# Loading wq on 128 partitions in two DMAs, and cutting each of the two last wo loads into four DMAs, in a decode attention kernel

## The chip, the core and the metric

The kernel runs on one core of a Trainium2 chip. The metric is the device time of one execution in microseconds (us); smaller is better. The core has a matrix engine (TensorE, PE in the profile, with its weight loads as PEld), a vector engine (VectorE, DVE), a scalar engine (ScalarE, ACT), GpSimd (POOL) and SyncE (SP), which here only issues DMAs. The engines run independently and meet at semaphores. Sixteen DMA engines carry the data from the memory of the chip (HBM) into the on-chip memory (SBUF, 128 partitions).

## What is computed

One decoding step: one token attends over a cache of 65,536 positions with 8 key/value heads and 16 query heads of 256 numbers each, and the result is mixed with a small token-mixing MLP by a sigmoid gate.

```python
g = sigmoid((x * gate_w).sum(-1))                # x: 1 x 1 x 448
q = (x @ wq).reshape(1, 1, 16, 256)              # wq: 448 x 4096
k, v = repeat(k_cache, 2), repeat(v_cache, 2)    # caches: 1 x 8 x 65536 x 256
p = softmax(q @ k.T / 16)
a = (p @ v).reshape(1, 1, 4096) @ wo             # wo: 4096 x 448
b = gelu(layernorm(x).T @ w1 + b1) @ w2 + b2     # over the token axis, of length 1
out = g * a + (1 - g) * b
```

Everything is bfloat16. The two caches are 268 MB each, the rest is small: wq and wo are 3.67 MB each.

## The kernel before, in words

The caches are read as NP = 64 pieces, j = 0 to 63, eight to a key/value head (PPH = 8). A piece is 8.39 MB of keys (tile kring) and 8.39 MB of values (tile vbuf), each on 128 partitions with 128 rows of 256 numbers per partition. Inside a piece PE works in BODY = 8 chunks: `transposes` (L293) turns the keys around with an identity matrix into PSUM (kst), DVE (L551) and ACT (L649) copy them to ktT, `scores` (L313) multiplies them by the two queries of the head, ACT makes the exponentials pT (L638), and after the eight chunks `values` (L348) multiplies pT by the values.

**The order of the loads** is written by hand in SP's program (L222 to L263). SP issues one DMA after the other; each is spread over the DMA engines, and each DMA engine works through its share of the queued DMAs in order. First comes wq (L223), into the space of vbuf, which no values need yet. Then, for j = 0, the two halves of the keys; then SP waits until the queries and the layer norm are ready (s_q, s_hb, L242 and L243) because the first values overwrite wq and other early tiles; then the values, and a wo load (L255). For every later j, SP waits until PE has transposed the first four chunks of the piece before (L232), issues keys j, waits until PE has finished with values j-1 (L245), and issues values j. The last piece comes in smaller DMAs: keys in two halves, values in rows 0 to 96, 96 to 112, 112 to 124 and 124 to 128. Each of these has its own semaphore. After them SP issues the two last wo loads (L258 to L260), one for each query head of the last key/value head: 128 partitions of two wo rows, 1,792 bytes per partition. SP then waits for the result (s_fin) and stores it.

**ACT's queue** issues the small loads at the start (L618 to L623): x, gate_w, w1, b1 and w2 (14 rows of 256 bytes each), and the single number b2.

**The start on the engines.** PE spreads x over partitions with four matmuls (L416), so that xcol[p, j] is x[4p + j]; this fits wq_a, in which partition p holds the four wq rows 4p to 4p+3, on PQ = 112 partitions. PE then waits for the small loads (L418), turns w1, b1 and w2 around (L419), DVE copies the result (L499, L500), and PE computes the queries with 16 x 2 groups of four matmuls (L428). DVE's layer norm and gate (L474 to L513) run beside it; DVE finishes with hbT (L588), which lets SP issue the first values.

**The end.** PE's `tail` (L401) adds the last value rows in `late_values`, waits for oTn from DVE, and then, for each of the two heads h, waits for that head's wo load (L408) and multiplies (L395, `project`). DVE adds up the output (L613) and SP stores it (L262).

Of the kernel before, what the change touches and what calls it, by code (L numbers as in the profile page):

```python
# [12 lines left out]
def bass_gated_mix__gqa_block_cached__mixer_token_mlp__decode_kernel(  # L13
# [14 lines left out]
    bf16 = mybir.dt.bfloat16  # L28
# [4 lines left out]
    DH = A_k_cache.shape[3]  # L33
    DM = A_x.shape[-1]
# [3 lines left out]
    FT = F // 128  # L38
    P = 128
    NQ = HQ * DH  # L40
# [13 lines left out]
    KTB = 2  # L54
    assert T % (CH * BODY) == 0 and PPH >= 2


    WF = 4
    PQ = DM // WF
    assert PQ * WF == DM and PQ <= P and PQ % 16 == 0  # L60

    NFIRST = 96
    NLATE = 112
    pieces = [(NFIRST, NLATE), (NLATE, 124), (124, NV)]


    NCG = 4
# [22 lines left out]
    with ctx:  # L92
        def sb(shape, dt, name):
            return ctx.enter_context(nc.sbuf_tensor(name, shape, dt))

        def psum(shape, dt, name):
            return ctx.enter_context(nc.psum_tensor(name, shape, dt))

        def new_sem(name):
            return ctx.enter_context(nc.semaphore(name))  # L100
# [9 lines left out]
        ident = sb([P, P], f32, "ident")  # L110
        ones_sq = sb([P, P], bf16, "ones_sq")

        wo_sb = sb([P, REP, 2 * DM], bf16, "wo_sb")
# [6 lines left out]

        early = vbuf[:, :, :].rearrange("p n d -> p (n d)")
        early_f = vbuf_f[:, :, :].rearrange("p n d -> p (n d)")
        wq_a = early[0:PQ, 0:WF * NQ].rearrange("p (j n) -> p j n", j=WF)
        used = [WF * NQ]

        def scratch(rows, n, dt=bf16):
            o = used[0]
            used[0] += n if dt == bf16 else 2 * n
            assert used[0] <= NV * DH and n % 2 == 0
            return early[0:rows, o:o + n] if dt == bf16 else early_f[0:rows, o // 2:o // 2 + n]  # L130

        wrows_b = scratch(3 * FT, P)
        identb = scratch(3 * FT, 3 * FT)
        xrow_b = scratch(1, DM)
        grow_b = scratch(1, DM)
        xcb_row = scratch(1, DM)
# [4 lines left out]
        scr_row = scratch(1, DM, f32)  # L141
        gu = sb([P, DM], bf16, "gu")
        w2cur = sb([P, 1], bf16, "w2cur")
        xcol = sb([PQ, WF], bf16, "xcol")
        oTn = sb([P, 2 * REP], bf16, "oTn")
        accs = sb([P, SELC], f32, "accs")
        sel = sb([P, REP], f32, "sel")
# [7 lines left out]
        params = sb([P, 3 * FT], f32, "params")  # L155
# [14 lines left out]
        sps = psum([P, 2, 512], f32, "sps")  # L170
        acc = psum([P, 512], f32, "acc")
# [8 lines left out]
        sem_wq = new_sem("sem_wq")  # L180
        sem_wo = new_sem("sem_wo")
        sem_wl = [new_sem("sem_wl%d" % h) for h in range(REP)]
# [6 lines left out]
        s_par = new_sem("s_par")  # L189
# [5 lines left out]
        s_d2a = new_sem("s_d2a")  # L195
        s_a2d = new_sem("s_a2d")
        s_col = new_sem("s_col")
        s_identb = new_sem("s_identb")
        s_xcol = new_sem("s_xcol")
        s_hrow = new_sem("s_hrow")  # L200
        s_h = new_sem("s_h")
# [14 lines left out]
        def src(cache, j, n0=0, n1=NV):  # L216
            g, m = divmod(j, PPH)
            s = cache[0, g, m * BODY * CH:(m + 1) * BODY * CH, :].rearrange("(p n) d -> p n d", p=P)
            return s[:, n0:n1, :].rearrange("p n d -> p (n d)")

        @block.sync
        def _(eng):  # L222
            eng.dma_start(wq_a.rearrange("p j n -> p (j n)"),  # L223
                          A_wq.rearrange("(p j) n -> p (j n)", j=WF)).then_inc(sem_wq, 16)
            def load(dst, cache, j, n0, n1, at, sem):
                eng.dma_start(dst[:, at + n0:at + n1, :].rearrange("p n d -> p (n d)"), src(cache, j, n0, n1)  # L226
                              ).then_inc(sem, 16)

            for j in range(NP):
                last = j == NP - 1  # L230
                if j >= 1:
                    eng.wait_ge(sem_tr[NB - 1], BODY * (j - 1) + DC)  # L232
                if j == 0:
                    load(kring, A_k_cache, j, HV, NV, 0, sem_k)
                    load(kring, A_k_cache, j, 0, HV, 0, sem_kb)
                elif last:
                    load(kring, A_k_cache, j, 0, HV, HV, sem_k)
                    load(kring, A_k_cache, j, HV, NV, HV, sem_kb)
                else:
                    load(kring, A_k_cache, j, 0, NV, HV * (j % 2), sem_k)  # L240
                if j == 0:
                    eng.wait_ge(s_q, 1)  # L242
                    eng.wait_ge(s_hb, 1)  # L243
                else:
                    eng.wait_ge(sem_pv, j)  # L245
                load(vbuf, A_v_cache, j, 0, NFIRST if last else NV, 0, sem_v)
                if last:
                    for (n0, n1), sem in zip(pieces, sem_vp):
                        load(vbuf, A_v_cache, j, n0, n1, 0, sem)
                g, m = divmod(j, PPH)  # L250
                if m == 0 and g < H - 1:
                    if g >= 1:
                        eng.wait_ge(s_proj, g)
                    w = A_wo[g * REP * DH:(g + 1) * REP * DH, :]
                    eng.dma_start(wo_rows, w.rearrange("(p i) n -> p (i n)", i=2 * REP)).then_inc(sem_wo, 16)  # L255

            eng.wait_ge(s_proj, H - 1)
            for h in range(REP):  # L258
                w = A_wo[(HQ - REP + h) * DH:(HQ - REP + h + 1) * DH, :]
                eng.dma_start(wo_sb[:, h, :], w.rearrange("(p j) n -> p (j n)", j=2)).then_inc(sem_wl[h], 16)  # L260
            eng.wait_ge(s_fin, 1)
            eng.dma_start(out_ap, out_g[0:P:P // NCG, :]).then_inc(sem_out, 16)  # L262
            eng.wait_ge(sem_out, 16)  # L263
# [13 lines left out]
        def _(pe):  # L277
            one = ones_sq[0:1, 0:1]
# [85 lines left out]
            def late_values(n0, n1):  # L364
                for n in range(n0, n1):
                    r, nt = divmod(n, NT)
                    piece_wait(n)
                    for dj in range(2):
                        ins = pe.matmul(sps[:, 0, dj * REP:(dj + 1) * REP], vbuf[:, n, dj:DH:2],
                                        pT[:, r, 2 * nt:2 * nt + 2], start=False,  # L370
                                        stop=(n == NV - 1), skip_group_check=True)
                return ins

            def by_d(dst):
                for dj in range(2):
                    ins = pe.matmul(dst[:, dj * REP:(dj + 1) * REP], accs[:, dj:DH:2], sel[:, :],
                                    start=(dj == 0), stop=True, skip_group_check=True)
                return ins
# [22 lines left out]
            def tail():  # L401
                pe.wait_ge(s_cp, H)
                by_d(sps[:, 0, 0:2 * REP])
                late_values(NLATE, NV).then_inc(s_late, 1)
                spin(1)
                pe.wait_ge(s_oTn, H)
                for h in range(REP):
                    pe.wait_ge(sem_wl[h], 16)  # L408
                    ins = project([dj * REP + h for dj in range(2)], 2 * h)
                ins.then_inc(s_proj, 1)  # L410

# [1 line left out]
            pe.wait_ge(sem_ident, 1)  # L413
            pe.wait_ge(sem_x, 16)
            for j in range(WF):
                pe.matmul(acc[0:PQ, j:j + 1], xrow_b[0:1, j:DM:WF], one, start=True, stop=True)  # L416
            pe.wait_ge(s_identb, 1)
            pe.wait_ge(sem_misc, 16 * 5)  # L418
            pe.matmul(acc[:, WF:WF + 3 * FT], wrows_b, identb, start=True, stop=True).then_inc(s_col, 1)  # L419

            pe.wait_ge(s_xcol, 1)
            pe.wait_ge(sem_wq, 16)
            for dj in range(2):
                for h in range(HQ):
                    j = dj * HQ + h
                    col = h * DH
                    for kt in range(WF):
                        ins = pe.matmul(sps[:, 1, j:j + 1], wq_a[:, kt, col + dj:col + DH:2],  # L428
                                        xcol[:, kt:kt + 1], start=(kt == 0), stop=(kt == WF - 1))
            ins.then_inc(s_q, 1)  # L430
            pe.wait_ge(s_hrow, 1)
            pe.matmul(prj[:, 0:DM], ones_sq[0:1, :], h_row, start=True, stop=True)  # L432
# [10 lines left out]
            with nc.Fori(0, H, 1, engines=on, head_slot={pe.engine: 0}) as g:  # L443
                with nc.Fori(0, PPH, 1, engines=on, head_slot={pe.engine: 0}) as m:
                    j = pe.snap(g * PPH + m, min_val=0, max_val=NP - 1)
# [19 lines left out]
        def _(vec):  # L465
            for b in range(0, NB, 2):
                vec.sem_inc(sem_ev[b], 1)
            vec.memset(zrow[:, :], 0.0)
            vec.wait_ge(sem_ident, 1)
            vec.tensor_copy(identb, ident[0:3 * FT, 0:3 * FT]).then_inc(s_identb, 1)  # L470
            vec.reduce_sum(sel[:, :], ident[:, :].rearrange("p (j n) -> p n j", j=4)[:, 0:REP, :], axis=AX.X)
            vec.wait_ge(sem_x, 16)
            vec.drain()
            vec.tensor_copy(xrow, xrow_b)  # L474
            vec.drain()
            vec.reduce_sum(stat[:, 0:1], xrow, axis=AX.X)
# [19 lines left out]
            vec.drain()  # L496
            vec.tensor_copy(statb[:, 4:5], stat[:, 3:4]).then_inc(s_d2a, 1)  # L497
            vec.wait_ge(s_col, 1)
            vec.tensor_copy(xcol[:, :], acc[0:PQ, 0:WF]).then_inc(s_xcol, 1)  # L499
            vec.tensor_copy(params[:, :], acc[:, WF:WF + 3 * FT]).then_inc(s_par, 1)  # L500
            vec.drain()
            vec.tensor_copy(w2p_b[:, :], params[:, 2 * FT:3 * FT])
            vec.wait_ge(s_a2d, 1)
# [87 lines left out]
            with nc.Fori(0, H - 1, 1, engines=on) as g:  # L591
                with nc.Fori(0, PPH, 1, engines=on) as m:
                    j = vec.snap(g * PPH + m, min_val=0, max_val=NP)
# [90 lines left out]
```

The softmax here doesn't subtract the row's maximum and nothing guards it: scores larger than these inputs give would overflow.

## Time and profile before

| | us |
|---|---|
| median of three executions | 1271.55 |
| lowest and highest of the three | 1271.47, 1271.93 |
| the profiled execution, its own time | 1271.93 |
| span of the profiled execution (first to last instruction) | 1270.1 |
| PE busy, of the span | 921.5 |
| ACT busy, of the span | 536.9 |
| DVE busy, of the span | 419.9 |
| HBM read | 544.22 MB, 428 GB/s over the span |

The profiled execution is the one that gave the highest of the three times; 1.8 us of its time lie outside its span. In the profile, L223 is line 223 of the kernel. A row "kring<-in_A_k_cache_dram" is a DMA from the key cache to the tile kring; "SPq" and "ACTq" are the issuing queues. The arrow in an idle time ("<-DMA ...") names what ended the wait. "Landing" is the arrival of a DMA's semaphore, which counts the DMA engines that have finished their share. The trace also keeps a record of each packet that a DMA engine moved (start, duration, size), and of each landing.

### The profile page before, as it was taken

The numbers are of one execution on the slowest core, as the hardware profiler recorded it, in microseconds if no ns is written. First come the engines' busy times: TensorE is split into PE (matmuls) and PEld (weight loads), VectorE is DVE, ScalarE is ACT, GpSimd is POOL, SyncE is SP. The second block draws the span as 40 slices with busy tenths as digits, with TensorE's granted clock in tenths as the row PEclk, the third lists the DMA queues.
The fourth block names the chain that finished last, engine by engine and source line by source line (L and its number), as shares of the span: only waits on it lengthen the run. The fifth ranks groups of instructions, "written<-read, shape, count | busy, mean of one in ns | idle before, by whom it ended". The sixth has DMA issues, their size and how long they took to land.

```text
span 1270.1 us, 38819 instructions
## 1 busy us (share of the span) xinstructions
PE 921.5 (73%) x17109; PEld 868.6 (68%) x17109; DVE 419.9 (33%) x752; ACT 536.9 (42%) x786; POOL 0.9 (0%) x7
## 2 busy tenths in 40 slices
PE   1776688666886667876677866769767688676798
PEld 1766688666786666776667866668766577666687
DVE  2323344333443334443223332223322233322233
ACT  0533355433454334554334543335533355433455
POOL 0000000000000000000000000000000000000000
PEclk9978898878887778988889888788878798878889
DMA  9999999999999999999999999999999999999998
GB/s 326 433 435 433 435 431 433 431 435 431 429 435 435 431 433 440 429 429 438 435 431 427 440 433 433 433 435 431 433 431 431 435 433 433 433 433 429 440 424 358
DMA packets 11470, 544.39 MB, mean 429 GB/s; under 512 B 1361, under 2 KB 1619, under 8 KB 2771
## 3 DMA queue, kind: packets, MB, share of 16 engines
q1 hardware_dynamic: 11368, 544.22, 99.7%
q8 instruction: 8, 0.13, 0.0%
q10 hardware_dynamic: 90, 0.01, 0.0%
q14 instruction: 4, 0.02, 0.0%
HBM read 544.22 MB, written 0.00 MB: 428 GB/s over the span
## 4 chain that ended last, share of the span: by engine, by line
DMA 69%; PE 29%; issue 1%; DVE 0%; ACTq 0%; SPq 0%; ACT 0%; DVEq 0%
DMA kring<-in_A_k_cache_dram 66%; PE kst L293 24%; PE sps L313 4%; DMA wo_sb<-in_A_wo_dram 2%; DMA b_b<-in_B_b_dram 2%; PE acc L348 0%; PE sps L428 0%; SPq L226 0%; ACTq L621 0%; DVE hbT L588 0%; DVE stat L495 0%; ACTq L618 0%; PE prj L432 0%; SPq L260 0%; DVE vbuf L493 0%
## 5 line engine op out<-in xcount | busy, mean ns | idle before, releaser
L649 ACT ACTIVATE ktT<-kst 128x1024 bf16<-128x1024 bf16 x512 | 499.1, 1021 | 662.4 <-PE kst L293 662.3
L293 PE MATMUL kst<-ident,kring 128*128 128x128 f32 x4096 | 559.7, 298 | 295.8 <-DMA kring<-in_A_k_cache_dram 284.6
L293 PEld LDWEIGHTS kst<-ident,kring 128*128 128x128 f32 x4096 | 509.8, 155 | 305.9 <-issue 303.2
L551 DVE COPY ktT<-kst 128x1024 bf16<-128x1024 bf16 x512 | 353.9, 692 | 756.4 <-PE kst L293 736.0
L313 PEld LDWEIGHTS sps<-qcur,ktT 128*128 128x128 bf16 x8192 | 237.7, 96 | 4.6 <-issue 2.1
L313 PE MATMUL sps<-qcur,ktT 128*128 128x2 bf16 x8192 | 236.6, 163 | 1.6 <-issue 1.5
L348 PE MATMUL acc<-vbuf,pT 128*2 128x256 bf16 x4080 | 148.9, 316 | 2.3 <-issue 1.5
L348 PEld LDWEIGHTS acc<-vbuf,pT 128*2 128x2 bf16 x4080 | 109.6, 96 | 33.0 <-issue 2.0
L638 ACT ACTIVATE pT<-sps 128x32 f32 x256 | 51.8, 202 | 16.6 <-PE sps L313 16.6
L337 PE MATMUL acc<-pT,ones_sq 128*128 128x32 bf16 x256 | 11.7, 178 | 12.3 <-ACT pT L638 12.3
L337 PEld LDWEIGHTS acc<-pT,ones_sq 128*128 128x128 bf16 x256 | 8.6, 97 | 15.2 <-ACT pT L638 14.9
L556 DVE COPY accs<-acc 128x288 f32<-128x288 f32 x8 | 3.7, 458 | 41.8 <-PE acc L348 41.8
L655 ACT ACTIVATE z_b<-z_b 128x448 bf16<-128x448 bf16 x14 | 8.1, 577 | 20.4 <-DVE z_b L538 20.4
L419 PE MATMUL acc<-vbuf 42*128 42x42 bf16 x1 | 0.2, 190 | 20.0 <-DMA b_b<-in_B_b_dram 20.0
L419 PEld LDWEIGHTS acc<-vbuf 42*128 42x128 bf16 x1 | 0.1, 102 | 20.0 <-issue 20.0
L384 PEld LDWEIGHTS acc<-sel,accs 128*64 128x64 f32 x112 | 10.8, 214 | 0.9
L384 PE MATMUL acc<-sel,accs 128*64 128x1 f32 x112 | 11.4, 260 | 0.0
L628 ACT ACTIVATE statb<-statb 1x1 bf16<-1x1 bf16 x1 | 0.2, 204 | 19.2 <-DVE statb L497 19.2
L493 DVE TENSOR_TENSOR vbuf<-vbuf 1x448 bf16<-1x448 bf16 x1 | 0.4, 381 | 16.8 <-DMA b_b<-in_B_b_dram 16.8
L544 DVE TENSOR_TENSOR gu<-wtmp,z_b 128x448 bf16<-128x448 bf16 x14 | 5.5, 393 | 1.0
L532 DVE TENSOR_TENSOR z_b<-wtmp,u_b 128x448 bf16<-128x448 bf16 x14 | 5.5, 393 | 1.0
L530 DVE TENSOR_TENSOR wtmp<-u_b 128x448 bf16<-128x448 bf16 x14 | 5.5, 392 | 1.1
(78 smaller groups left out, 81.1 us busy)
## 6 DMA issues: line engine op xcount, KB each, us to landing
kring<-in_A_k_cache_dram SPq DMA_DIRECT2D x4, 4096.0 KB, 27.2
vbuf<-in_A_v_cache_dram SPq DMA_DIRECT2D x1, 6144.0 KB, 24.7
vbuf<-in_A_wq_dram SPq DMA_DIRECT2D x1, 3584.0 KB, 17.5
wo_sb<-in_A_wo_dram SPq DMA_DIRECT2D x7, 448.0 KB, 27.2
vbuf<-in_A_v_cache_dram SPq DMA_DIRECT2D x1, 1024.0 KB, 26.9
vbuf<-in_A_v_cache_dram SPq DMA_DIRECT2D x1, 768.0 KB, 28.3
vbuf<-in_A_v_cache_dram SPq DMA_DIRECT2D x31, 29.7
kring<-in_A_k_cache_dram SPq DMA_DIRECT2D x30, 27.6
```

What stands on the lines that cost most here:

```text
L293: ins = pe.transpose(kst[:, b, i * P:(i + 1) * P], kring_f[:, at + NT * (k % DC) + 4 * b + i, :], ident[:, :])
L313: ins = pe.matmul(sps[:, par, 2 * nt:2 * nt + 2], ktT[:, par, b, ntl * DH + dj:(ntl + 1) * DH:2], qcur[:, dj, :], start=(dj == 0), stop=(d ...
L337: pe.matmul(acc[:, DENC:SELC], ones_sq[:, :], pT[:, r, :], start=False, stop=(r == BODY - 1), skip_group_check=True)
L348: ins = pe.matmul(acc[o:o + REP, 0:DH], pT[:, r, 2 * nt:2 * nt + 2], vbuf[:, n, :], start=False, stop=False, skip_group_check=True)
L384: ins = pe.matmul(dst[hh * HP:(hh + 1) * HP, i:i + 1], accs[:, i:DH:2 * REP], sel[:, hh:hh + 1], start=False, stop=True, skip_group_check= ...
L530: vec.tensor_tensor(W, U, U, op=ALU.mult)
L532: vec.tensor_tensor(Z, W, U, op=ALU.mult)
L544: vec.tensor_tensor(gu[:, :], W, Z, op=ALU.mult).then_inc(s_pb, 1)
L551: vec.tensor_copy(ktT[:, k % KTB, b, :], kst_b[:, b, :]).then_inc(sem_ev[b], 1)
L638: act.activation(pT[:, bass.ds(p0 + k % DC, 1), :].rearrange("p o n -> p (o n)"), sps[:, k % 2, 0:2 * NT], AF.Exp, scale=scale).then_inc(s ...
L649: act.activation(ktT[:, k % KTB, b, :], kst_b[:, b, :], AF.Copy).then_inc(sem_ev[b], 1)
L655: act.activation(z_b[:, :], z_b[:, :], AF.Tanh).then_inc(s_tanh, 1)
```

## The change

Two parts of the load program are different.

- **wq.** In place of one DMA to 112 partitions of four rows each, two DMAs: rows 0 to 383 go to 128 partitions of three rows each (wq_a, 24,576 bytes per partition), and the 64 rows that are left go to 128 partitions of half a row each (wq_b, 4,096 bytes per partition). A half row holds the columns of eight heads, so that each query head uses either the even or the odd partitions of wq_b: x is laid out for that in two more columns of xcol, with zeros on the other partitions. DVE fills a row xrem for this (one memset, two copies), PE spreads it with two more matmuls, and the fourth matmul of each group reads wq_b in place of the fourth row of wq_a. PE waits for both DMAs (32 in place of 16 on sem_wq).
- **wo.** Each of the two last wo loads is cut at partitions 96, 121 and 126 into four DMAs of 96, 25, 5 and 2 partitions. They run on 16, 5, 5 and 2 of the DMA engines, where the uncut load runs on 16 with 8 partitions each. All four count on the same semaphore, and PE waits for 64.

```diff
-    WF = 4
-    PQ = DM // WF
+    WF = 3
+    REM = DM - WF * P
+    HALF = NQ // 2
...
+    wo_cuts = [(0, 96), (96, 121), (121, 126), (126, P)]
...
-        wq_a = early[0:PQ, 0:WF * NQ].rearrange("p (j n) -> p j n", j=WF)
+        wq_a = early[:, 0:WF * NQ].rearrange("p (j n) -> p j n", j=WF)
+        wq_b = early[:, WF * NQ:WF * NQ + HALF]
+        xrem = scratch(1, 2 * P).rearrange("p (a n) -> p a n", a=2)
...
             eng.dma_start(wq_a.rearrange("p j n -> p (j n)"),
-                          A_wq.rearrange("(p j) n -> p (j n)", j=WF)).then_inc(sem_wq, 16)
+                          A_wq[0:WF * P, :].rearrange("(p j) n -> p (j n)", p=P)).then_inc(sem_wq, 16)
+            eng.dma_start(wq_b, A_wq[WF * P:DM, :].rearrange("r (a n) -> (r a) n", a=2)
+                          ).then_inc(sem_wq, 16)
...
                 w = A_wo[(HQ - REP + h) * DH:(HQ - REP + h + 1) * DH, :]
-                eng.dma_start(wo_sb[:, h, :], w.rearrange("(p j) n -> p (j n)", j=2)).then_inc(sem_wl[h], 16)
+                rows = w.rearrange("(p j) n -> p (j n)", j=2)
+                for p0, p1 in wo_cuts:
+                    eng.dma_start(wo_sb[p0:p1, h, :], rows[p0:p1, :]).then_inc(sem_wl[h], 16)
...
-                    pe.wait_ge(sem_wl[h], 16)
+                    pe.wait_ge(sem_wl[h], 16 * len(wo_cuts))
...
             for j in range(WF):
-                pe.matmul(acc[0:PQ, j:j + 1], xrow_b[0:1, j:DM:WF], one, start=True, stop=True)
-            pe.wait_ge(s_identb, 1)
+                pe.matmul(acc[:, j:j + 1], xrow_b[0:1, j:WF * P:WF], one, start=True, stop=True)
+            pe.wait_ge(s_xrem, 2)
+            for a in range(2):
+                pe.matmul(acc[:, WF + a:WF + a + 1], xrem[0:1, a, :], one, start=True, stop=True)
...
-            pe.wait_ge(sem_wq, 16)
+            pe.wait_ge(sem_wq, 32)
...
                     for kt in range(WF):
-                        ins = pe.matmul(sps[:, 1, j:j + 1], wq_a[:, kt, col + dj:col + DH:2],
-                                        xcol[:, kt:kt + 1], start=(kt == 0), stop=(kt == WF - 1))
+                        pe.matmul(sps[:, 1, j:j + 1], wq_a[:, kt, col + dj:col + DH:2],
+                                  xcol[:, kt:kt + 1], start=(kt == 0), stop=False)
+                    ins = pe.matmul(sps[:, 1, j:j + 1], wq_b[:, cb + dj:cb + DH:2],
+                                    xcol[:, WF + a:WF + a + 1], start=False, stop=True)
...
+            vec.memset(xrem, 0.0)
...
-            vec.tensor_copy(identb, ident[0:3 * FT, 0:3 * FT]).then_inc(s_identb, 1)
+            vec.tensor_copy(identb, ident[0:3 * FT, 0:3 * FT]).then_inc(s_xrem, 1)
...
+            vec.tensor_copy(xrem[0:1, 0, 0:P:2], xrow_b[0:1, WF * P:DM])
+            vec.tensor_copy(xrem[0:1, 1, 1:P:2], xrow_b[0:1, WF * P:DM]).then_inc(s_xrem, 1)
...
-            vec.tensor_copy(xcol[:, :], acc[0:PQ, 0:WF]).then_inc(s_xcol, 1)
+            vec.tensor_copy(xcol[:, :], acc[:, 0:WF + 2]).then_inc(s_xcol, 1)
```

More of the change, by code (lines that the diff above doesn't have):

```diff
@@ L55, in bass_gated_mix__gqa_block_cached__mixer_token_mlp__decode_kernel @@
     assert T % (CH * BODY) == 0 and PPH >= 2
-    WF = 4
-    PQ = DM // WF
-    assert PQ * WF == DM and PQ <= P and PQ % 16 == 0
+    WF = 3
+    REM = DM - WF * P
+    assert 0 < REM and 2 * REM == P
+    HALF = NQ // 2
     NFIRST = 96
@@ L122, in bass_gated_mix__gqa_block_cached__mixer_token_mlp__decode_kernel @@
         early_f = vbuf_f[:, :, :].rearrange("p n d -> p (n d)")
-        wq_a = early[0:PQ, 0:WF * NQ].rearrange("p (j n) -> p j n", j=WF)
-        used = [WF * NQ]
+        wq_a = early[:, 0:WF * NQ].rearrange("p (j n) -> p j n", j=WF)
+        wq_b = early[:, WF * NQ:WF * NQ + HALF]
+        used = [WF * NQ + HALF]
         def scratch(rows, n, dt=bf16):
@@ L143, in bass_gated_mix__gqa_block_cached__mixer_token_mlp__decode_kernel @@
         w2cur = sb([P, 1], bf16, "w2cur")
-        xcol = sb([PQ, WF], bf16, "xcol")
+        xcol = sb([P, WF + 2], bf16, "xcol")
         oTn = sb([P, 2 * REP], bf16, "oTn")
@@ L197, in bass_gated_mix__gqa_block_cached__mixer_token_mlp__decode_kernel @@
         s_col = new_sem("s_col")
-        s_identb = new_sem("s_identb")
+        s_xrem = new_sem("s_xrem")
         s_xcol = new_sem("s_xcol")
@@ L415, in _ @@
             for j in range(WF):
-                pe.matmul(acc[0:PQ, j:j + 1], xrow_b[0:1, j:DM:WF], one, start=True, stop=True)
-            pe.wait_ge(s_identb, 1)
+                pe.matmul(acc[:, j:j + 1], xrow_b[0:1, j:WF * P:WF], one, start=True, stop=True)
+            pe.wait_ge(s_xrem, 2)
+            for a in range(2):
+                pe.matmul(acc[:, WF + a:WF + a + 1], xrem[0:1, a, :], one, start=True, stop=True)
             pe.wait_ge(sem_misc, 16 * 5)
-            pe.matmul(acc[:, WF:WF + 3 * FT], wrows_b, identb, start=True, stop=True).then_inc(s_col, 1)
+            pe.matmul(acc[:, WF + 2:WF + 2 + 3 * FT], wrows_b, identb, start=True, stop=True).then_inc(s_col, 1)
             pe.wait_ge(s_xcol, 1)
-            pe.wait_ge(sem_wq, 16)
+            pe.wait_ge(sem_wq, 32)
             for dj in range(2):
@@ L426, in _ @@
                     col = h * DH
+                    a, cb = divmod(col, HALF)
                     for kt in range(WF):
-                        ins = pe.matmul(sps[:, 1, j:j + 1], wq_a[:, kt, col + dj:col + DH:2],
-                                        xcol[:, kt:kt + 1], start=(kt == 0), stop=(kt == WF - 1))
+                        pe.matmul(sps[:, 1, j:j + 1], wq_a[:, kt, col + dj:col + DH:2],
+                                  xcol[:, kt:kt + 1], start=(kt == 0), stop=False)
+                    ins = pe.matmul(sps[:, 1, j:j + 1], wq_b[:, cb + dj:cb + DH:2],
+                                    xcol[:, WF + a:WF + a + 1], start=False, stop=True)
             ins.then_inc(s_q, 1)
@@ L498, in _ @@
             vec.wait_ge(s_col, 1)
-            vec.tensor_copy(xcol[:, :], acc[0:PQ, 0:WF]).then_inc(s_xcol, 1)
-            vec.tensor_copy(params[:, :], acc[:, WF:WF + 3 * FT]).then_inc(s_par, 1)
+            vec.tensor_copy(xcol[:, :], acc[:, 0:WF + 2]).then_inc(s_xcol, 1)
+            vec.tensor_copy(params[:, :], acc[:, WF + 2:WF + 2 + 3 * FT]).then_inc(s_par, 1)
             vec.drain()
```

## The prediction

> **What bounds the kernel now.** I read the page from the top. Its slices by time come first:
>
> ```profile
> PEclk9978898878887778988889888788878798878889
> DMA  9999999999999999999999999999999999999998
> GB/s 326 433 435 433 435 431 433 431 435 431 429 435 435 431 433 440 429 429 438 435 431 427 440 433 433 433 435 431 433 431 431 435 433 433 433 433 429 440 424 358
> ```
>
> The DMA engines are busy in every slice of 31.75 us and move about 433 GB/s in each, while PE is busy 73% of the span. So the kernel is bound by the stream of loads, and its time is the start of the stream, plus the bytes at the rate, plus what follows the last landing. The first slice is odd: as busy as the others, but at 326 GB/s. The busy times by stretch resolve it (columns: stretch, its length, busy time of each engine with its instructions, PE clock, DMA share, GB/s):
>
> ```profile
> 2.00:15.00 13.00, 0.55 (x4) 0.49 (x4) 3.10 (x12) 1.28 (x1) 0.00 (x0) 1.00 0.98 253
> 15.00:18.00 3.00, 0.00 (x0) 0.00 (x0) 0.00 (x0) 0.00 (x0) 0.00 (x0) 1.00 0.84 252
> 18.00:30.00 12.00, 4.88 (x133) 3.97 (x133) 3.43 (x16) 1.69 (x3) 0.00 (x0) 1.00 1.00 431
> ```
>
> From 2 to 18 us the engines are occupied but run at 253 GB/s; from 18 us on they run at 431. The slow stretch is the wq load. In the trace's packet records, wq is 112 packets of 32,768 bytes, seven to an engine, started at 1.76 to 14.82 us, mean 2.03 us each. The first keys, which follow on the same engines, have packets of the same size: 1.22 us each. Key packets begun before 17.2 us are still slow, those begun after 17.6 us are not; wq's sixteen landings run from 16.35 to 18.20 us. The slow phase ends when the last wq data is in. The chain of work that ended last shows the other places that the change touches:
>
> ```profile
> 2.79 19.71 DMA b_b<-in_B_b_dram
> ...
> 29.20 9.82 issue
> 39.03 5.98 PE kst L293 x32
> ...
> 1238.99 28.37 DMA wo_sb<-in_A_wo_dram
> 1267.36 0.04 issue
> 1267.40 0.30 PE prj L395 x8
> ```
>
> b2 (2 bytes) lands at 22.49 us, and PE's first matmuls on keys begin at 39.03; but neither holds up the loads. At the end the second of the two last wo loads lands last, at 1267.36.
>
> [...] 32,768 bytes in 1.22 us is 26.9 GB/s per engine. [...] The trace of before has only 16 landings for each large load[...].
>
> **wq, the load.** Per engine the bytes stay 229,376: eight packets of 24,576 and eight of 4,096 in place of seven of 32,768. Packets of 2,048, 6,144, 8,192 and 32,768 bytes took 84, 238, 313 and 1,218 ns to 128 partitions, which is about 11 ns plus 36.8 ns per KiB, so 0.90 to 0.92 us for 24 KiB and 0.16 for 4 KiB. Sum: 8 x (0.915 + 0.16) = 8.6 us. Before: 7 x 2.03 = 14.2 us, and then the slowed key packets. The whole loss by another way: bytes moved up to 19 us in the packet records are 4.61 MB; at 432 GB/s from 1.9 us on they need 10.7 us, and they took 17.1, so 6.4 us are lost. The first slice gives a lower value: 31.75 us x 326 = 10.35 MB, which need 24.0 us of 29.85, a loss of 5.8. The two stretches of 253 and 252 GB/s give 16 us x (1 - 253/431) = 6.6. I take 6.4, less 0.1 for the smaller packets. The end belongs to the slowest engine, not to the mean; the engines left the slow phase within about 1.0 us of each other, and some that come last at the end (those that carry instruction fetches later) were 0.3 ahead of the mean there. So I take 6.3 - 0.4 = **5.9 us**. Bounds if the rate is right: 5.4 and 6.7.
>
> **Does the gain reach the end?** Only if no ring of loads runs dry. SP issues the first values at 28.87, the first of the next keys at 50.21 and the next values at 73.85. The rings would run dry at about 35.4, 55.9 and 75 (first landing of the load ahead, less 1 us); with the stream 6 us earlier at 29.5, 50 and 69. All three issues must therefore move too. They hang on b2 and on wq. b2's packets alternate on one engine with about a dozen bulk packets; with 0.92 and 0.16 us in place of 2.03 and 1.22 I estimate 10 to 11 us for its landing. wq lands at 1.9 + 8.6 + 0.6 = 11.1. Before, wq's matmuls to the first values' issue took 23.92 to 28.87, b2 to that issue 6.4; so the issue comes at 16 to 17.5. PE's start then follows at 9.8 us (the "issue" row, which I leave as long) at some 27, next keys at 38, next values at 62: covers of 12, 12 and 7 us. If that cover were gone because PE's start stayed at 39, next keys would be issued at 50.2 and up to 1.3 us would be lost again.
>
> **wq, the rest.** One more DMA on SP, 0.41 us, delays the first keys' issue (1.21 to 1.62): zero, since the wq packets fill the engines until 10. PE: five spreading matmuls for four (0.14 us each), in a wait for b2; query matmuls stay 128. DVE: one memset (0.18, as L468) and two copies (0.14 to 0.2 each) before a chain that ended at 5.7 us and then idled for 16.8; the new wait s_xrem on PE is met near 3 us, and behind it stand only the waits for b2 and wq. Zero, with 4 us of cover left at b2 = 10.
>
> **wo.** SP issues eight DMAs in place of two at the end: 8 x 0.42 = 3.4 us in place of 0.9. Nothing is queued behind them but the store, and their data is wanted 25 us later: zero. Data: a row of 1,792 bytes took 75 ns. Per engine 8 rows become 6, plus five and one on five engines and one more on two of these: over both loads 16 rows become 12 (-0.30 us) on eleven engines, 24 (+0.60) on three and 26 (+0.75) on two; the extra semaphore packets are 9 ns each. The landings of the last wo load before spread over 2.35 us: two at 1265.01 and 1265.16, three at 1265.63 to 1265.69, eleven from 1265.94 to 1267.36. If the five with more rows are the five early ones, they end at 1265.8 to 1266.3, and the last landing becomes 1267.06. Then the cover shows: PE is busy with the first head until 1267.18 and would start the second at about 1267.2 instead of 1267.40. Gain 0.2. If the five are not the early ones, up to +0.75. Which engines are early cannot be read off the profile with certainty[...]. I take **-0.2**.
>
> **Sum.** 5.9 + 0.2 = 6.1 us off the profiled execution's span: 1270.1 becomes 1264.0, its own time 1271.93 becomes 1265.8. The median is 0.4 below the profiled execution: 1265.4.
>
> **The rivals.**
> - **Cold start.** The memory or the engines are slow for the first 17 us whatever is loaded. For it: the first keys' packets, already on 128 partitions, are slow as well until 17.6, and all engines become fast together. Against it: the change comes just when the last wq data lands. Then only the wo part is left: 1271.3, 1272.3 if it goes wrong.
> - **Half.** wq runs at an intermediate rate, as it did near 10 us, when packets took 1.53 us (343 GB/s): 3.67 MB then take 10.7 us, the gain is 4.0 or less: 1267.5 to 1269.
> - **Shared ports for good.** [...] 229,376 bytes at 13.5 GB/s are 17.0 us. wq would end at 18.9 instead of 17.65: 1272.8, up to 1275 if the slow rows hold up b2 and the first values too. It decides from the point where a 24,576-byte packet takes over 1.6 us. Against it: the keys' 128-partition loads run at 431 right after.
>
> **Numbers.** Full gain 0.70 (1264.2 to 1267), half 0.10, cold start 0.14, shared ports 0.06. The first two hold 8 in 10: range 1264.2 to 1269. A difference of 0.2%, 2.5 us, is about what a measurement tells from none. Faster by more: 0.80; within: cold start and half of the shared ports, 0.17; slower: 0.03.
>
> **What would show it.** Right: 2 to 10 us at over 400 GB/s, wq's landings near 11, first values issued before 18, next keys before 40, the stretch after at 431 to 435 as now, the last wo landings closer together. Wrong: packets of 24,576 bytes at 1.4 us or more; a gap in the DMA share before 80 us; a last wo landing later than its neighbours.

## The result, and the profile after

The changed kernel takes 1267.26 us in the median (six executions, 1266.95 to 1267.74) against 1271.70 for the kernel before (1271.47 to 1271.93): 4.4 us less, a ratio of 0.9965 with a 95% interval from 0.9952 to 0.9978. The profiled execution went from 1271.93 to 1267.47 us, its span from 1270.1 to 1265.3. So 4.46 us were gained where 6.1 were forecast. The direction and the place of the gain were right; one of the two parts of the change does the opposite of what was forecast for it.

The slices of the page of the changed kernel (GB/s in 40 equal parts of the span):

```profile
DMA  9999999999999999999999999999999999999998
GB/s 410 427 434 433 433 433 435 433 433 433 433 431 435 435 431 435 429 435 435 435 431 429 435 435 435 435 429 431 435 435 435 431 433 431 435 433 435 433 427 348
```

The first slice has risen from 326 to 410, the middle stands at 433 as before, and the last slice has fallen from 358 to 348. A gain at the start, and something at the end. The stretches of the start, same columns as before. First one of the kernel before, then three of the changed kernel:

```profile
4.00:10.00 6.00, 0.00 (x0) 0.00 (x0) 1.48 (x6) 0.59 (x1) 0.00 (x0) 1.00 0.93 241
```

```profile
2.00:4.00 2.00, 0.42 (x5) 0.29 (x5) 1.62 (x9) 0.71 (x1) 0.00 (x0) 1.00 0.59 221
4.00:10.00 6.00, 0.00 (x0) 0.00 (x0) 1.69 (x6) 0.57 (x1) 0.00 (x0) 1.00 0.96 409
18.00:30.00 12.00, 2.58 (x12) 2.58 (x13) 0.69 (x1) 0.51 (x1) 0.00 (x0) 1.00 1.02 434
```

wq now loads at over 400 GB/s from 4 us on, where it was 241; only the stretch from 2 to 4 us is slow. The issues of SP that feed the stream (start, duration, line, DMA), first of the kernel before, then of the changed kernel:

```profile
28.87 0.33 SPq L226 DMA_DIRECT2D vbuf<-in_A_v_cache_dram  x1
...
50.21 0.33 SPq L226 DMA_DIRECT2D kring<-in_A_k_cache_dram  x1
73.85 0.33 SPq L226 DMA_DIRECT2D vbuf<-in_A_v_cache_dram  x1
```

```profile
0.73 0.42 SPq L229 DMA_DIRECT2D vbuf<-in_A_wq_dram  x1
1.22 0.40 SPq L231 DMA_DIRECT2D vbuf<-in_A_wq_dram  x1
1.67 1.07 SPq L234 DMA_DIRECT2D kring<-in_A_k_cache_dram  x2
17.35 0.33 SPq L234 DMA_DIRECT2D vbuf<-in_A_v_cache_dram  x1
...
37.79 0.33 SPq L234 DMA_DIRECT2D kring<-in_A_k_cache_dram  x1
61.51 0.33 SPq L234 DMA_DIRECT2D vbuf<-in_A_v_cache_dram  x1
```

First values at 17.35 instead of 28.87, next keys at 37.79 instead of 50.21, next values at 61.51 instead of 73.85: all three moved far enough that no ring (kring or vbuf, whose space is filled again and again) ran dry, that is, the DMA engines never ran out of issued loads. They move 435 GB/s from 30 to 60 us and 431 from 60 to 120. The end of the chain of work that ended last:

```profile
1232.02 29.68 DMA vbuf<-in_A_v_cache_dram
1261.69 0.05 issue
1261.74 0.35 PE sps L379 x8
1262.09 0.24 PE kst L339
1262.33 0.02 issue
1262.35 0.52 PE prj L405 x16
```

Before, the last wo load ended the chain. Now the last four value rows do (1261.69), and wo does not hold PE up: its two loads land at 1262.10 and 1262.49, and PE multiplies by the first from 1262.35 on. The value rows 96 to 112, whose packets are all through before the first wo packet, land 5.52 us earlier than before (1258.15 against 1263.67). But from there to the end of the span it takes 7.16 us, where it took 6.46 (by the trace's spans of 1265.31 and 1270.13 us; with spans rounded to 0.1 us the figures are 7.15 and 6.43). That is where part of the gain went.

The pieces use as many engines as the change says: each of the two wo loads has 28 landings near the end in the changed kernel (16 + 5 + 5 + 2), and 16 in the kernel before. SP's eight issues took longer than the recorded 3.4 us:

```profile
1232.49 6.13 SPq L270 DMA_DIRECT2D wo_sb<-in_A_wo_dram  x8
```

The last of them alone took 3.60 us. They still lie 20 us ahead of the data, so this cost nothing here.

### The profile page after: what moved, and what is told of

Its sections match the earlier page's. It is cut to its first block, busy times and chain, and to the rows that moved or that the text cites. A ratio compares the mean times of both kernels' runs of the same rounds, so it can differ in the third digit from the quotient of the medians.

```text
span 1265.3 us, 38830 instructions
## 1 busy us (share of the span) xinstructions
PE 916.9 (72%) x17110; PEld 866.5 (68%) x17110; DVE 420.5 (33%) x755; ACT 537.2 (42%) x786; POOL 0.9 (0%) x7
## 4 chain that ended last, share of the span: by engine, by line
DMA 70%; PE 28%; issue 1%; SPq 0%; DVE 0%; ACT 0%; ACTq 0%
DMA kring<-in_A_k_cache_dram 68%; PE kst L303 24%; PE sps L323 4%; DMA vbuf<-in_A_v_cache_dram 2%; PE acc L358 0%; SPq L234 0%; PE prj L405 0%; SPq L229 0%; SPq L231 0%; PE acc L347 0%; PE sps L379 0%; DVE out_g L631 0%; PE kst L339 0%; ACT pT L656 0%; ACTq L656 0%
## 5 line engine op out<-in xcount | busy, mean ns | idle before, releaser
L358 PE MATMUL acc<-vbuf,pT 128*2 128x256 bf16 x4080 | 143.7, 309 | 2.4 <-issue 1.7
L554 DVE TENSOR_TENSOR z_b<-u_b,wtmp 128x448 bf16<-128x448 bf16 x14 | 5.5, 392 | 1.0
L560 DVE TENSOR_SCALAR z_b<-z_b 128x448 bf16<-128x448 bf16 x14 | 3.9, 277 | 5.5 <-ACT z_b L673 5.5
```

Of the source, the lines that this page charges most:

```text
L358: ins = pe.matmul(acc[o:o + REP, 0:DH], pT[:, r, 2 * nt:2 * nt + 2], vbuf[:, n, :], start=False, stop=False, skip_group_check=True)
L554: vec.tensor_tensor(Z, U, W, op=ALU.add)
```

## The experiments

Two theories were put against each other. **Ports:** a load that is not laid out over all 128 partitions is slow, and slows whatever else is in flight; this makes wq on 112 partitions slow, and the cut wo loads too. Its name is the author's guess at the reason; no record here shows a port. **Rivals:** the start is slow (cold) whatever is loaded; or it is the number and size of the DMAs; or the memory side of wq. Times below are medians beside runs of the kernel before on the same chip; ratios are to that kernel.

### 1. wq alone

```diff
-    wo_cuts = [(0, 96), (96, 121), (121, 126), (126, P)]
+    wo_cuts = [(0, P)]
```

> The changed kernel with its two last wo loads left whole (128 partitions, one DMA each); wq as changed. Theory 'ports': [...] slow the value packets still in flight, which cost 0.7 us of span in the changed kernel (from the landing of value rows 96 to 112 to the end of the span: 6.43 us before, 7.15 after). Then this kernel keeps the 5.5 us that the loads were early before the tail: span 1264.5, time 1266.2 to 1266.6. Rival 'wq gave less, the cuts are neutral or a gain': time as the changed kernel or up to 0.3 more, 1267.3 to 1267.6.

Measured: 1266.58 us (1266.44 to 1266.68), ratio 0.9957 (0.9944 to 0.9971); span 1264.4. So it is wq that gives the whole gain, and without the cuts the kernel is 0.7 us faster than with them; the executions of the two, measured in different series, do not overlap (the changed kernel took 1266.95 or more). This version beats both kernels. What the cuts do shows in the microseconds in which the last value rows and the wo loads cross. First the changed kernel, then this one (last two columns: DMA share and GB/s):

```profile
1258.00:1259.00 1.00, 0.94 (x36) 0.56 (x24) 0.01 (x1) 0.00 (x0) 0.00 (x0) 1.00 1.04 336
1259.00:1260.00 1.00, 0.50 (x4) 0.50 (x4) 0.80 (x3) 0.00 (x0) 0.00 (x0) 1.00 0.95 226
1260.00:1261.00 1.00, 0.34 (x10) 0.26 (x10) 0.00 (x0) 0.00 (x0) 0.00 (x0) 1.00 0.75 179
1261.00:1262.00 1.00, 0.80 (x31) 0.72 (x27) 0.00 (x0) 0.00 (x0) 0.00 (x0) 1.00 0.34 106
```

```profile
1258.00:1259.00 1.00, 0.74 (x28) 0.39 (x20) 0.20 (x1) 0.00 (x0) 0.00 (x0) 1.00 1.00 383
1259.00:1260.00 1.00, 0.69 (x8) 0.65 (x9) 0.60 (x3) 0.00 (x0) 0.00 (x0) 1.00 0.76 281
1260.00:1261.00 1.00, 1.00 (x33) 0.81 (x32) 0.09 (x1) 0.00 (x0) 0.00 (x0) 1.00 0.36 131
1261.00:1262.00 1.00, 0.65 (x17) 0.23 (x16) 0.08 (x1) 0.00 (x0) 0.00 (x0) 1.00 0.01 4
```

With the cuts the engines are busier and move less: 0.95 busy at 226 GB/s, against 0.76 at 281. The packet records name the victims. With whole loads, value packets of 6,144 bytes took at most 246 ns and wo packets of 1,792 bytes 76 in the median and 93 at most. With the cuts: up to 382 ns for the values, whose own DMA is unchanged, and 111 in the median and up to 255 for wo. The last value rows land 2.53 us after the rows 96 to 112 with whole loads, and 3.54 us after them with the cuts.

### 2. The cuts alone

The diff of the wo part, put into the kernel before; wq stays on 112 partitions.

> The kernel before with only the two last wo loads cut into 96, 25, 5 and 2 partitions; wq on 112 partitions as before. Theory 'ports': the cuts cost 0.7 to 1.1 us wherever they stand: 1272.4 to 1272.8, with packets of 6,144 bytes of the late values at up to 380 ns instead of 246. The recorded step (the five early engines take the extra rows): 1271.5. Rival 'the cuts only hurt because the changed kernel's early engines are others': 1271.5 too, with value packets at their old durations.

Measured: 1273.05 us (1272.22 to 1274.19), beside 1271.91; ratio 1.0007 (1.0000 to 1.0014). The interval just touches no difference, so the trace has to decide: value packets of 6,144 bytes took up to 487 ns (246 without cuts), those of 2,048 up to 282 (94). The last value rows land 3.35 us after the rows 96 to 112; without cuts it was 2.52. The cuts cost about 1 us here too, so it is not the changed kernel's wq that makes them costly. The recorded step gave -0.2. The theory had the sign and the victims right, and the size too small: the time is 0.25 us above its range, and the slowest value packet well above its 380 ns.

### 3. As many DMAs, every piece on all 128 partitions

```diff
-    wo_cuts = [(0, 96), (96, 121), (121, 126), (126, P)]
+    wo_cuts = [(0, 672), (672, 847), (847, 882), (882, 896)]
...
-                    eng.dma_start(wo_sb[p0:p1, h, :], rows[p0:p1, :]).then_inc(sem_wl[h], 16)
+                    eng.dma_start(wo_sb[:, h, p0:p1], rows[:, p0:p1]).then_inc(sem_wl[h], 16)
```

> The changed kernel, but each of the two last wo loads is cut into four DMAs along its columns (672, 175, 35 and 14 of 896 numbers), each on all 128 partitions: as many DMAs and semaphore increments on SP as in the changed kernel[...]. Theory 'ports': value packets of 6,144 bytes stay below 250 ns; the small pieces cost about 0.3 us a load (60 + 24 + 14 + 12 = 110 ns a partition for 75), so 1266.5 to 1267.0. Rival 'the number of DMAs costs, or their semaphores': value packets slow as in the changed kernel, 1267.3 or more.

Measured: 1267.44 us (1267.08 to 1267.77), ratio 0.9964 (0.9951 to 0.9978). As a time it is a miss, 0.4 above the range, and it falls where the rival put it: cut in this way the kernel is no faster than the changed one. The two are told apart by the packets: values of 6,144 bytes took at most 246 ns, those of 2,048 at most 94, and the last value rows land 2.59 us after the rows 96 to 112, all as with whole loads. So the eight DMAs and their semaphores slowed no other load here; they have a price of their own. The pieces took 63, 23, 12 and 9 ns a partition in the mean, 107 where a whole row took 77. Over both loads (16 packets of each piece an engine) that is 0.5 us, and by 0.5 the profiled span is longer than with whole loads. The profiled execution is one of the quickest, though; by the medians the price is 0.9, and the rest of that is not explained.

SP's issues show something that was not expected:

```profile
1232.88 23.83 SPq L270 DMA_DIRECT2D wo_sb<-in_A_wo_dram  x8
```

Alone, such an issue takes some 0.43 us; here the fifth took 11.49 and the sixth 6.62. What SP waits for is not in the records. The last was out at 1256.70, before the first packet of any wo piece (1257.86), so it did not delay the data.

### 4. Two pieces, of 96 and 32 partitions

```diff
-    wo_cuts = [(0, 96), (96, 121), (121, 126), (126, P)]
+    wo_cuts = [(0, 96), (96, P)]
```

> The changed kernel with the two last wo loads cut into 96 and 32 partitions only[...]. Theory 'ports': [...] value packets are slowed as in the changed kernel, time 1266.9 to 1267.5. Rival 'the pieces on five and two engines are the cost': the value packets are at their old durations and the time is that of whole loads, 1266.2 to 1266.6.

Measured: 1267.61 us (1267.12 to 1267.74), ratio 0.9964 (0.9951 to 0.9978), 1.0 above whole loads in the same series. Value packets of 6,144 bytes took up to 399 ns and wo packets 104 in the median. The last value rows land 3.69 us after the rows 96 to 112. So two pieces of 96 and 32 partitions cost as much as the four. They were meant to put six and two rows on each of sixteen engines, eight as uncut; on how many engines the piece of 32 ran is not shown here. Nor was the memory side tried apart: with other pieces, an engine may also read other rows of wo. Its rates in the crossing are those of the changed kernel:

```profile
1258.00:1259.00 1.00, 0.83 (x32) 0.47 (x20) 0.12 (x1) 0.00 (x0) 0.00 (x0) 1.00 1.06 336
1259.00:1260.00 1.00, 0.61 (x4) 0.55 (x4) 0.69 (x3) 0.00 (x0) 0.00 (x0) 1.00 0.94 227
```

### 5. Is the start cold, or is it wq?

```diff
-            eng.dma_start(wq_a..., A_wq...).then_inc(sem_wq, 16)
...
                     load(kring, A_k_cache, j, HV, NV, 0, sem_k)
+                    eng.dma_start(wq_a..., A_wq...).then_inc(sem_wq, 16)
                     load(kring, A_k_cache, j, 0, HV, 0, sem_kb)
```

> The kernel before with one change of order: the first half of the first keys (128 partitions, packets of 32,768 bytes) is loaded ahead of wq (112 partitions, packets of the same size). Theory 'ports': the keys run at 1.22 us a packet from the second packet on, and wq's packets take about 2 us each wherever they stand, here from 11 to 26 us; the time is that of the kernel before, 1271.5 to 1272.3. Rival 'cold start': the first 15 us are slow whatever is loaded, so the keys' packets take about 2 us and wq's, later, about 1.2.

Measured, stretches of this kernel:

```profile
4.00:10.00 6.00, 0.00 (x0) 0.00 (x0) 1.71 (x6) 0.68 (x1) 0.00 (x0) 1.00 1.02 438
12.00:16.00 4.00, 0.00 (x0) 0.00 (x0) 0.00 (x0) 0.00 (x0) 0.00 (x0) 1.00 1.08 262
...
74.00:80.00 6.00, 5.13 (x99) 3.15 (x99) 0.00 (x0) 0.00 (x0) 0.00 (x0) 0.56 0.42 178
```

The keys, first in line, run at 438 GB/s; wq, from 12 us on, at 262. The packets agree: keys 1.21 us each, wq's 2.07 in the mean (1.49 to 2.40), as at the start of the kernel before. The slowness goes where wq goes, so the cold start falls as its cause. A small part of it is real: where the first load lies on 128 partitions, the first packet of an engine was slow, here 1.70 us in the mean in place of 1.21. With wq on 112 partitions in front, as in the kernel before, it does not stand out (1.95, and 2.03 for all of wq's).

The time was a miss, 3.7 us above the range: 1276.00 us (1275.67 to 1276.31), ratio 1.0027 (1.0017 to 1.0038). The last line shows where it went. wq lands at 28.59 here, first values are issued at 33.66, PE begins on keys at 44.92, and the next values are issued only at 79.60, after the keys ahead of them had landed: from 74 to 80 us the engines are busy 42%. The rings ran dry, at the very place where the kernel before had a cover of only a microsecond or so (issued at 73.85, needed at about 75). Cover is the time by which an issue comes before the engines would run out of loads.

### 6. wq on 64 partitions

```diff
-    WF = 4
+    WF = 7
```

(Three rows of scratch also move into tiles of their own, to make room.)

> The kernel before with wq on 64 partitions of seven rows (WF = 7, four partitions to an engine; three rows of scratch moved out of the values' tile to make room). Theory 'ports': [...] packets of 57,344 bytes take 4.25 us, 13.5 GB/s an engine, and wq ends at about 19.5, 1.3 us later than before; time 1273.0, up to 1275 if the slow packets hold up b2 and with it the first values. Rival 'the slow phase is the memory's side of wq, or the start': the bytes and their order in memory are the same, so the same 15 to 17 GB/s an engine, 3.4 to 3.8 us a packet, and 1271.9.

Measured, one stretch of this kernel:

```profile
12.00:16.00 4.00, 0.00 (x0) 0.00 (x0) 0.00 (x0) 0.00 (x0) 0.00 (x0) 1.00 1.05 215
```

wq's packets of 57,344 bytes took 4.48 us in the mean after the first, 12.8 GB/s an engine; those of 112 partitions had 15 to 17, those of 128 have 26.9. The theory said 13.5, half of 26.9, the rival 15 to 17. Since the same bytes are read in the same order as in the kernel before, the memory side alone does not set the rate. The run gives about half the rate (12.8 of 26.9); why, it does not show. The time was a miss, far above the range: 1282.56 us, ratio 1.0079 (1.0065 to 1.0092). wq lands at 22.34, b2 at 27.29, first values are issued at 38.24, and again the rings ran dry (85% busy from 60 to 100 us).

### 7. Two DMAs and short packets, still on 112 partitions

```diff
-            eng.dma_start(wq_a.rearrange("p j n -> p (j n)"),
-                          A_wq.rearrange("(p j) n -> p (j n)", j=WF)).then_inc(sem_wq, 16)
+            eng.dma_start(wq_flat[:, 0:3 * NQ], wq_rows[:, 0:3 * NQ]).then_inc(sem_wq, 16)
+            eng.dma_start(wq_flat[:, 3 * NQ:4 * NQ], wq_rows[:, 3 * NQ:4 * NQ]).then_inc(sem_wq, 16)
```

> The kernel before with wq in two DMAs (three rows and one row of each partition's four), still on 112 partitions: packets of 24,576 bytes as in the changed kernel, but shares of seven partitions. Theory 'ports': slow as before, about 1.5 us a packet of 24,576 and 0.5 of 8,192, time 1271.9 to 1272.6. Rival 'two DMAs or shorter packets are what made wq fast': 0.92 us a packet, time near 1266.5. Beside it: kernels with wq on 128 partitions have 2.17 to 2.23 us of their time outside the span, kernels without it 1.77 to 1.85; if the second DMA is the cause, this kernel has about 2.2.

Measured: 1271.63 us beside 1271.75, ratio 0.9998 (0.9990 to 1.0007), 0.3 below the range and no gain. One stretch:

```profile
4.00:10.00 6.00, 0.00 (x0) 0.00 (x0) 1.47 (x6) 0.70 (x1) 0.00 (x0) 1.00 0.99 259
```

Packets of 24,576 bytes took 1.50 us in the mean after the first, on 128 partitions 0.91. The packet size and the number of DMAs are those of the changed kernel, so neither is what made wq fast; what differs is the partition count, and with it the rows that a packet carries.

### 8 to 10. The time outside the span

In the changed kernel 2.16 us of the profiled execution's time lie outside its span, before 1.80. The kernels of experiments 1, 3 and 4, with wq on 128 partitions, show 2.16 to 2.20, those of experiments 2, 5, 6 and 7 1.80. (The expectations have 1.83 and 2.17 from spans rounded to 0.1 us.) Experiment 7 had the second DMA, so it is not that. Experiment 8 puts only the work for xrem into the kernel before (DVE's memset and two copies, PE's two matmuls, results unread), 9 moves the memset to POOL in the kernel of experiment 1, 10 puts only the memset into the kernel before.

```diff
+            vec.memset(xrem, 0.0)
...
+            vec.tensor_copy(xrem[0:1, 0, 0:P:2], xrow_b[0:1, 3 * P:DM])
+            vec.tensor_copy(xrem[0:1, 1, 1:P:2], xrow_b[0:1, 3 * P:DM]).then_inc(s_identb, 1)
...
+            for a in range(2):
+                pe.matmul(acc[:, WF + 3 * FT + a:WF + 3 * FT + a + 1], xrem[0:1, a, :], one, start=True, stop=True)
```

> The kernel before with only the changed kernel's additions on the engines: xrem's memset and two copies on DVE, and two more matmuls on PE, whose results nobody reads; wq's load as before. Both the recorded working and its rivals: nothing, 1271.5 to 1272.3, since these lie beside the wait for b2. Beside it: if the longer programs of DVE or PE are what adds 0.35 us outside the span, this kernel has about 2.2 us there, otherwise about 1.83.

> The changed kernel with whole wo loads (as e1_wq_only), and the memset of xrem moved from DVE to POOL, ahead of its wait-free start. Theory 'DVE's memset adds the 0.35 us outside the span': outside 1.83, time 1266.2. Rival 'the copies or PE's two matmuls add it': outside 2.15 to 2.2, time 1266.4 to 1266.7 as e1_wq_only. Either way it should not be slower than the changed kernel.

> The kernel before with one more DVE memset (xrem, which nobody reads) ahead of the others. Theory 'DVE's memset adds it': outside 2.15 and time 0.3 above before, near 1272.1. Rival 'the copies or PE's matmuls': outside 1.83, time as before.

| | time | ratio | time of the profiled execution outside its span |
|---|---|---|---|
| 8, all of xrem's work | 1272.22 | 0.9999 (0.9990 to 1.0007) | 2.16 |
| 9, memset on POOL, whole wo | 1266.41 | 0.9957 (0.9943 to 0.9970) | 2.03 |
| 10, memset alone | 1271.74 | 1.0000 (0.9992 to 1.0009) | 1.80 |

So the 0.36 us come, for the most part at least, with the two copies or the two matmuls: the second DMA adds nothing, nor does the memset alone. With the memset on POOL in place of DVE 0.13 of them are gone, which neither theory had said. Which instructions it is, and where outside the span the time lies, stays open; in the medians the amount is too small to be told from nothing.

## Why the prediction was right, and where it was wrong

By the recorded sum, on the profiled executions:

| term | forecast | measured | from |
|---|---|---|---|
| wq's load | -5.9 | -5.52 | landing of value rows 96 to 112 |
| cut wo loads | -0.2 | +0.70 | from that landing to the end of the span, 6.46 to 7.16 |
| time outside the span | 0 | +0.36 | 1.80 to 2.16 |
| sum | -6.1 | -4.46 | 1271.93 to 1267.47 |

- **What bounds the kernel** held. The middle of the stream runs at 433 GB/s in both kernels, and what was gained at the start arrived at the end, 1,240 us later, less what the tail took back.
- **wq: the mechanism was right.** Packets of 24,576 bytes take 0.912 us (forecast 0.90 to 0.92) and those of 4,096 0.159 (0.16). The size was off in two places that partly cancel. The 6.4 us of loss were all put down to wq, but slow first packets remain when wq is fast, 1.70 us in the mean in place of 0.91. At 19 us, against 432 GB/s from 1.9 us on, the stream before had lost 6.47 us and the changed one has lost 0.97, so 5.50 were there to gain. And the allowance of 0.4 for late engines was not needed. Because of the slow first packets the forecast sign "2 to 10 us at over 400 GB/s" came true only from 4 us on.
- **The covers** held with numbers: b2's wait ends at 10.98 (forecast 10 to 11), wq's last landing is at 12.20 (11.1, but PE can use it only from 12.4 on), first values are issued at 17.35 (16 to 17.5), PE's start at 27.43 (27), next keys 37.79 (38), next values 61.51 (62). Experiments 5 and 6 show what happens when they do not: 4 and 10 us lost against the kernel before.
- **wo: this step failed.** It read: "If the five with more rows are the five early ones, they end at 1265.8 to 1266.3, and the last landing becomes 1267.06." It took 75 ns a row from the whole loads, for a load on 96 partitions, and called the wrong engines the only danger (+0.75). But the same prediction had started from a load on 112 partitions that ran at 15 to 17 GB/s an engine, where those on 128 had 26.9; it did not ask whether pieces of 96, 25, 5 and 2 would be slow too. Experiment 4 shows that pieces of 96 and 32 cost as much as the four: in the changed kernel wo's packets rise from 76 to 111 ns in the median, and the value packets beside them become slow too, which delays PE's last values. The last landing that matters became that of a value load. Nor were the extra pieces free in themselves, as experiment 3 shows. The landings of the last wo load did not come closer together: they spread over 2.16 us, where they spread over 2.35 before and 2.21 with wq alone changed. That the pieces of 25, 5 and 2 share the same few engines was the author's assumption: landings count engines and do not name them. Whether these are the early ones was not tried.
- **The rest of wq at zero** was right within the span. The 0.36 us outside it came from a part priced at nothing.
- **The rivals.** Cold start: rejected by experiment 5, except for the first packet of each engine. Half: not seen. Shared ports for good, in figures half of 26.9 GB/s an engine all through: not in wq on 128 partitions (0.912 us a packet; that rival began at 1.6); on 64 partitions, in experiment 6, the packets have nearly the rate that was said (12.8 GB/s, forecast 13.5).
- **The range and luck.** The time of 1267.26 lies inside the stated range, but 0.3 above its main part, "full gain" (1264.2 to 1267). The room above was made for wq at half the gain, which did not happen; the miss on wo used it up. That much of the range was luck. wq alone (1266.58) lies in the main part.

Shown is that wq's speed goes with its partition layout, wherever it stands in the stream and in packets of either size: 128 partitions 26.9 GB/s an engine, 112 about 16, 64 12.8. The reason is not in the records. On 112 partitions wq took 14.2 us an engine (7 packets of 2.03), and all engines were slow about alike, with landings from 16.35 to 18.20. Why the value packets of experiment 4 became slow beside the cut wo loads, no run here shows.

## What to carry to other kernels

In a kernel bound by its loads, look for a stretch in which the DMA engines are busy but move less than elsewhere (here 241 GB/s at a share of 0.93, where later it was 431), and compare packets of the same size in and out of it. Where the slow load does not cover all 128 partitions, lay the data out again so that it does, even at the price of a second DMA and some extra work on idle engines; here wq went from 241 to 409 GB/s. Do not cut a small last load to balance the engines: cut along its partitions, the pieces and the loads beside them were slow here (values up to 382 ns for 246); cut along its columns, the other loads were spared (246), but the kernel was no faster than with the first cut (1267.44 us, 1267.26). Whole loads were the best of the three (1266.58).

## What the runs showed that was not expected

- A load cut along its partitions slowed others. With wo on 96 and 32 partitions, value packets of 6,144 bytes whose own DMA was untouched took up to 399 ns instead of at most 246.
- Where the first load lies on 128 partitions, the first packet of an engine cost in the mean 0.5 to 0.8 us more than the next ones: 1.70 us for 24,576 bytes in place of 0.91, 1.70 for 32,768 in place of 1.21.
- SP's issues took long. With eight pieces on 128 partitions behind the last value loads, the eight issues took 23.83 us in place of some 3.4 (experiment 3).
- A memset, two tiny copies and two tiny matmuls beside a long wait moved the time outside the span from 1.80 to 2.16 us.
